# Decay attention and a two-layer product in one kernel: the order of a job's second product, the distance of a unit's second product, and the queues of loads and stores

## The chip, the cores and the metric

The kernel runs on one core of a Trainium2 chip. The core has five engines, each with an instruction stream of its own that it works through strictly in order: TensorE (PE in the profile; its weight loads are listed apart as PEld), VectorE (DVE), ScalarE (ACT), GpSimd (POOL) and SyncE (SP), which here only issues transfers. Engines wait for each other through semaphores. Transfers are issued by an engine's queue and carried out by 16 DMA engines. The metric is the time of one execution in microseconds (us), lower is better.

## What is computed

The first half is attention with a decay, for 8 batches and 8 heads, 576 positions and a head size of 64; the second half is a two-layer product on the attention's output, with a piecewise quadratic between the layers.

```python
# q, k, v: (8, 8, 576, 64)   f: (8, 8, 576)
scores = np.matmul(q, k.transpose(0, 1, 3, 2)) / np.sqrt(D)
cum = np.cumsum(np.log(np.clip(f, 0.0001, 1.0)), axis=-1)
decay = cum[:, :, :, None] - cum[:, :, None, :]
scores = np.where(causal, -1e9, scores + decay)
attn = softmax(scores)                       # over the last axis
x = np.matmul(attn, v)                       # -> (4608, 512), heads side by side
h = x @ w_in                                 # (4608, 2048)
g = np.where(h >= 1, h, np.where(h <= -1, 0.0, (h + 1) ** 2 / 4))
out = g @ w_out                              # (4608, 512)
```

Inputs and outputs are float32. The kernel splits most operands of its matmuls into a high and a low float16 part and sums three products, high by high, low by high and high by low.

## The kernel before, in words

**Jobs.** The attention is cut into 36 jobs. A job is two heads of one batch and a range of query tiles of 128 rows. Batch 0 has eight jobs, four with the tiles 0 and 1 and four with the tiles 2 to 4; each of the other seven batches has four jobs with all five tiles (28 jobs). The first 12 jobs (`NQK`) and the first 5 (`NPE`) take simpler paths for scores and for weights; what follows is the general one.

- `load` (L326) brings the queries and keys of a job's two heads into one of two buffers, `qk32[ji % 2]` (L347, L351). `load_decay` (L355) brings the running sums of the decay, `ck` (L358).
- `measure` (L390) sums the squares of queries and keys on ACT (L397) and turns them into scales by a tiny matmul (L128) and a few VectorE instructions.
- `prepare` (L408) makes the float16 parts `qs` on ACT (L414) and VectorE (L416), which reads the buffer for the last time, and turns them by a DMA transpose (L421) into `qkT`.
- `scores` (L459) multiplies one query tile with all its keys (L482); POOL makes the decay and the causal mask (L488, L492).
- `weights` (L557) adds, takes the exponential and the sum (L571, L575), divides and splits into `pr` (L589, L595), and turns `pr` by DMA transposes into the job's `pT` (L601; L604 for the last tile). `pT` has one buffer.
- `split_values` (L427) brings the job's values into `v32` (L440, L442) and makes their float16 parts `vs` (L447, L448), in two buffers.
- `values` (L608), the job's second product, multiplies `pT` with `vs` (L615) and writes the result into `x` (L624, L625).

**The loop** (from L759) opens job p with the load of pair p+2, prepares pair p+1 and computes the scores of the first tile. Then come the steps. A step (L773) computes the scores of the next tile and the weights of this one; the last but one also brings the next job's values, the last one measures pair p+2. The second product of job p-1 is a step of its own, `finish` (L794), put in by hand: at place 4 where the job has five tiles, which is behind four tiles, otherwise at place 2.

**Units.** The two-layer product runs in units of 256 tokens by 256 hidden columns, 18 chunks of tokens with 8 units each. `moe_front` (L642) makes 24 to 48 matmuls into `ph` (L657), and then `u` and `g`: L666 and L667 on ACT, L668 on VectorE, L670 on ACT, L671 on VectorE. `moe_back` (L678) makes the second product, twelve matmuls into the two halves of `po` (L685); after the last unit of a chunk `po` is copied to `ot` (L702) and stored (L705). `ph` and `g` have two buffers each, the halves of `po` one each. `moe_unit` (L710) emits the front of a unit and the back of the unit before. Units are spread over the steps of a job by a quota.

**The order on each engine.** The program is written down in the order above, but the launch code builds it with `schedule_with_timeline_sim=True`: a scheduler simulates it at build time, and puts on each engine's stream what its own times see ready first, the earlier written one where several are ready. An engine's stream is therefore fixed at build, with later jobs' instructions moved ahead into gaps. On the chip an engine still takes it strictly in order. SP's queue holds all transfers, stores included.

Of the kernel before, what the change touches and what calls it, by code (L numbers as in the profile page):

```python
# [8 lines left out]
F32 = mybir.dt.float32  # L9
F16 = mybir.dt.float16  # L10
I32 = mybir.dt.int32
AF = mybir.ActivationFunctionType
ALU = mybir.AluOpType
AX = mybir.AxisListType

P = 128
# [29 lines left out]
def kernel(  # L46
# [19 lines left out]
    nc = tc.nc  # L66

    B, H, S, D = q.shape
    DM, DF = w_in.shape
    NPAIR = H // 2  # L70
    NT5 = -(-S // P)
# [6 lines left out]
    TC = 256  # L78
    NCH = B * S // TC
    jobs = [(b, hp, r0, r1) for b in range(B) for r0, r1 in CUTS.get(b, ((0, NT5),)) for hp in range(NPAIR)]  # L80
    njobs = len(jobs)
# [65 lines left out]
    def decay_sums():  # L147
        fl = early
        nb = B * H
        nc.sync.dma_start(fl[0:nb, 0:S], f.rearrange("b h s -> (b h) s"))  # L150
        nc.vector.tensor_scalar(
            out=fl[0:nb, 0:S], in0=fl[0:nb, 0:S], scalar1=1e-4, scalar2=1.0, op0=ALU.max, op1=ALU.min
        )
        nc.scalar.activation(fl[0:nb, S:2 * S], fl[0:nb, 0:S], AF.Ln)
        nc.gpsimd.memset(fl[0:nb, 3 * S:4 * S], 0.0)
        cum = fl[0:nb, 2 * S:3 * S]
        nc.vector.tensor_tensor_scan(
            out=cum, data0=fl[0:nb, S:2 * S], data1=fl[0:nb, 3 * S:4 * S], initial=0.0, op0=ALU.add, op1=ALU.add
        )
        nc.sync.dma_start(cum_d, cum)  # L160
        pt = ps.tile([P, 1024], F32, name="s")
        twice = fl[0:nb, 0:P]
        nc.vector.tensor_copy(
            twice.rearrange("p (a b) -> p a b", a=2), cum[:, FULL:S].unsqueeze(1).broadcast_to([nb, 2, 64])
        )
        for t in range(NT5):
            nc.tensor.transpose(
                pt[:, nb * t:nb * t + nb], cum[:, P * t:P * t + P] if t < LAST else twice, ident[0:nb, 0:nb]
            )
        nc.vector.tensor_copy(cq.rearrange("p t n -> p (t n)"), pt[:, 0:NT5 * nb])  # L170

# [193 lines left out]
    early_qk = [two.tile([P, 4, SP], F16, name="qkT") for i in range(2)]  # L367
    early_qk = [t.rearrange("p c s -> p (c s)").bitcast(F32)[:, 0:2 * S].rearrange("p (c s) -> p c s", c=2) for t in early_qk]
    squares = bits.bitcast(F16)[:, 0:2 * NT5 * D]
    cq8 = const.tile([P, NT5, 2 * H], F32, name="cq8")  # L370

    def early_prepare(w):

        if w.p == 0:
            nc.vector.tensor_scalar(out=cq8, in0=cq[:, :, 0:2 * H], scalar1=8.0, scalar2=None, op0=ALU.mult)
        t_ = early_qk[(w.p + NQK) % 2]
        w.nsig, w.nalpha = -8.0, -0.125
        bh = w.b * H + 2 * w.hp
        w.cqs = cq8[:, :, bh:bh + 2]
        w.terms = ((t_[:, 0], t_[:, 1]),)  # L380
        for j in range(2):
            pt = ps.tile([P, 1024], F32, name="s")
            t0 = 0 if j else w.r0
            n = w.s1 - P * t0
            for c0 in range(0, n, P):
                m = min(P, n - c0)
                nc.tensor.transpose(pt[:, c0:c0 + m], w.x32[j][0:m, c0:c0 + P], ident[0:m, 0:m])
            nc.scalar.activation(t_[:, j, 0:n], pt[:, 0:n], AF.Copy)

    def measure(w):  # L390

        if w.p < NQK:
            return
        bh = w.b * H + 2 * w.hp
        m2 = tiny.tile([P, 2], F32, name="m2q")
        for j in range(2):
            nc.scalar.activation(squares, w.x32[j], AF.Square, accum_out=m2[:, j:j + 1])  # L397
        w.sc = sc = tiny.tile([P, 2], F32, name="sc")
        pw = tiny.tile([P, 2], F32, name="pw")
        from_norms(sc, pw, m2)  # L400
        w.nsig = tiny.tile([P, 1], F32, name="nsig")
        nc.vector.tensor_scalar(out=w.nsig, in0=sc[:, 0:1], scalar1=sc[:, 1:2], scalar2=-8.0, op0=ALU.mult, op1=ALU.mult)
        w.nalpha = tiny.tile([P, 1], F32, name="nalpha")
        nc.vector.tensor_scalar(out=w.nalpha, in0=pw[:, 0:1], scalar1=pw[:, 1:2], scalar2=-0.125, op0=ALU.mult, op1=ALU.mult)
        w.cqs = tiny.tile([P, NT5, 2], F32, name="cqs")
        nc.vector.tensor_scalar(out=w.cqs, in0=cq[:, :, bh:bh + 2], scalar1=w.nsig, scalar2=-1.0, op0=ALU.mult, op1=ALU.mult)

    def prepare(w):  # L408
        if w.p < NQK:
# [232 lines left out]
    def moe_front(ch, fb):  # L642
        g0 = ch * TC
        b0 = g0 // S
        n0 = min(TC, (b0 + 1) * S - g0)
        segs = [(0, n0, b0, g0 - b0 * S)] + ([(n0, TC, b0 + 1, 0)] if n0 < TC else [])
        last = segs[-1][2]
        if (ch, fb) not in bsc and last not in bsc:
            bsc[last] = moe_scales(last)
        z = bsc.get((ch, fb)) or bsc[last]  # L650
        i = fb - z.first
        ph = ps.tile([P, 2, TC], F32, name="ph")
        for fi in range(2):
            for t in range(NKT):
                for wl, xl in ((0, 0), (0, 1), (1, 0)):
                    for a0, a1, b, s0 in segs:
                        nc.tensor.matmul(  # L657
                            ph[:, fi, a0:a1],
                            lhsT=wi[fb][:, wl, t, fi * P:(fi + 1) * P],
                            rhs=xs[b][:, t, xl, s0:s0 + a1 - a0],  # L660
                            start=(fi == 0 and t == 0 and wl == 0 and xl == 0 and a0 == 0),
                            stop=(fi == 1 and t == NKT - 1 and wl == 1 and a1 == TC),
                        )
        h = ph.rearrange("p f t -> p (f t)")
        u = two.tile([P, 2 * TC], F32, name="u")
        nc.scalar.activation(u, h, AF.Relu, scale=z.u[:, i:i + 1], bias=z.h[:, i:i + 1])  # L666
        nc.scalar.activation(u, u, AF.Square)  # L667
        nc.vector.scalar_tensor_tensor(out=u, in0=h, scalar=z.t[:, i:i + 1], in1=u, op0=ALU.max, op1=ALU.min)  # L668
        g = two.tile([P, 2, 2 * TC], F16, name="g")
        nc.scalar.activation(g[:, 0], u, AF.Copy, scale=z.r[:, i:i + 1])  # L670
        nc.vector.scalar_tensor_tensor(  # L671
            out=g[:, 1], in0=u, scalar=z.r[:, i:i + 1], in1=g[:, 0], op0=ALU.mult, op1=ALU.subtract
        )
        return ch, fb, g, z

    ots = {}

    def moe_back(ch, fb, g, z):  # L678
        first, last, part = z.first == fb, z.last == fb, z.first > 0
        if first:  # L680
            po[ch] = [ps1.tile([P, DM], F32, name=f"po{i}") for i in range(2)]
        for fi in range(2):
            for i in range(2):
                for gl, wl in ((0, 0), (0, 1), (1, 0)):
                    nc.tensor.matmul(  # L685
                        po[ch][i],
                        lhsT=g[:, gl, fi * TC + i * P:fi * TC + (i + 1) * P],
                        rhs=wo[fb][:, wl, fi, :],
                        start=(first and fi == 0 and gl == 0 and wl == 0),
                        stop=(last and fi == 1 and gl == 1),  # L690
                    )
        if not last:
            return
        if not part:
            ots[ch] = [two.tile([P, DM], F32, name="ot") for i in range(2)]
        for i in range(2):
            if part:
                nc.vector.scalar_tensor_tensor(
                    out=ots[ch][i], in0=po[ch][i], scalar=z.osc, in1=ots[ch][i], op0=ALU.mult, op1=ALU.add
                )  # L700
            else:
                nc.scalar.activation(ots[ch][i], po[ch][i], AF.Copy, scale=z.osc)  # L702
            if fb == NB - 1:
                tok = ch * TC + i * P
                nc.sync.dma_start(out[tok:tok + P, :], ots[ch][i])  # L705


    pending = []

    def moe_unit(ch, fb):  # L710
        pending.append(moe_front(ch, fb))
        if len(pending) > 1:
            moe_back(*pending.pop(0))

    units = [(ch, fb) for ch, first, end in EARLY for fb in range(first, end)]
# [40 lines left out]
        value_step(0, i)  # L756
    value_scale(0)
    split_values(pairs[0])
    for p in range(njobs + 1):  # L759
        w = pairs[p] if p < njobs else None  # L760
        nxt = pairs[p + 1] if p + 1 < njobs else None
        steps = []
        if w:
            if w.b not in xs:
                xs[w.b] = xpool.tile([P, NPAIR, 2, S], F16, name="x")
            if p + 2 < njobs:
                pairs.append(load(p + 2))
            if nxt:
                load_decay(nxt, 0)
                prepare(nxt)  # L770
# [2 lines left out]
            def step(r):  # L773
                if r + 1 < w.r1:
                    scores(w, r + 1)
                if r == w.r1 - 2 and nxt:
                    load_decay(nxt, 1)
                    split_values(nxt)
                weights(w, r)
                if w.r1 == NT5 and w.b + 1 < B:  # L780
                    n = w.r1 - w.r0
                    i = w.hp * n + r - w.r0 - (NPAIR - 1) * n + -(-(NPAIR + 1) // n) * n
                    if 0 <= i <= NPAIR:
                        value_step(w.b + 1, i)
                    if w.hp == NPAIR - 1 and r == w.r0:
                        value_scale(w.b + 1)
# [4 lines left out]
        if p > 0:  # L791
# [7 lines left out]
                        join_scales(wp.b - 1)  # L799
                    tokens = wp.b * S + wp.s1  # L800

            steps.insert(4 if len(steps) == NT5 else 2, finish)
        load_weights(LOADS.get(p, 0))
        blocks = CONVERT.get(p, 0)
        quota = -(-ready() // (NPAIR - (p + NPAIR - 1) % NPAIR))
# [45 lines left out]
```

## Time and profile before

| | us |
|---|---|
| median of 3 runs | 1209.1 (1208.8 to 1213.09) |
| the profiled execution | 1206.77 |
| its span, first to last instruction | 1205.0 |
| TensorE busy | 1047.8 (87%) |
| ACT busy | 795.6 (66%) |
| VectorE busy | 789.7 (66%) |
| GpSimd busy | 418.1 (35%) |

A row of the waits names the waiting engine, its tile and line, then who released it, the total in us, how often, and the longest. A row of the timeline has start, duration, engine, line, what is written from what, how many instructions were merged, and in brackets how long the engine stood before and who ended it. `SPq` is SP's queue, whose durations are the time that issuing took. Every slice of the page has the clock granted to TensorE in tenths of full speed: nine tenths or more after the first fifth of the span, six to nine tenths in it.

### The profile page before, as it was taken

How to read it: one execution, taken by the hardware profiler on the slowest of the kernel's cores; microseconds unless marked ns; L12 is line 12 of the kernel's file. 1: busy time of each engine (PE TensorE's matmuls, PEld its weight loads, DVE VectorE, ACT ScalarE, POOL GpSimd, SP SyncE). 2: the span in 40 equal slices, each digit the busy share in tenths (PEclk: the TensorE clock that was granted, in tenths of full speed). 3: DMA queues.
4: the chain of work that ended last, by engine and by line, in shares of the span. 5: the costliest groups of instructions: out<-in, count | busy, mean ns of one | idle time of the engine just before them, and what ended most of it. 6: DMA issues, size and time to landing. Idle time of an engine off the chain costs nothing. (4 is left out here: it accounts for less than half of the span.)

```text
span 1205.0 us, 24383 instructions
## 1 busy us (share of the span) xinstructions
PE 1047.8 (87%) x8809; PEld 664.8 (55%) x8809; DVE 789.7 (66%) x2103; ACT 795.6 (66%) x1638; POOL 418.1 (35%) x679
## 2 busy tenths in 40 slices
PE   4666765988978889898898998999898999999998
PEld 2433443554645556555655655555565566667665
DVE  5769989787767667765566666676677686532222
ACT  4566876577867677776566667777677686644443
POOL 4467764234533233333213323342343343100000
PEclk9666888998989999998999999999899999999999
DMA  7868788479857566854633745675668575300000
GB/s 226 271 173 243 166 208 180 111 160 181 170 118 169 113 134 127 155 112 111 126 69 76 144 87 130 117 155 116 129 127 149 106 139 105 73 19 1 18 18 18
DMA packets 408281, 152.18 MB, mean 126 GB/s; under 512 B 383968, under 2 KB 384992, under 8 KB 408160
## 3 DMA queue, kind: packets, MB, share of 16 engines
q1 hardware_dynamic: 408160, 150.63, 57.7%
q8 instruction: 69, 1.13, 0.4%
q14 instruction: 52, 0.43, 0.1%
HBM read 75.64 MB, written 9.58 MB: 71 GB/s over the span
## 5 line engine op out<-in xcount | busy, mean ns | idle before, releaser
L685 PE MATMUL po<-place,g 128*128 128x512 f16 x1728 | 429.5, 393 | 55.0 <-ACT g L670 39.4
L657 PE MATMUL ph<-x,place 128*128 128x256 f16 (+3 forms) x4608 | 420.7, 248 | 24.0 <-DVE u L668 24.0
L657 PEld LDWEIGHTS <-place 128*128 128x128 f16 x4608 | 354.2, 98 | 94.2 <-issue 38.5
L685 PEld LDWEIGHTS <-g 128*128 128x128 f16 x1728 | 165.0, 100 | 245.2 <-ACT g L670 56.3
L488 POOL TENSOR_SCALAR sdr<-ck,nsig,cqs 128x128 f32<-128x128 f32 (+1 forms) x192 | 147.3, 771 | 151.2 <-DVE pr L595 148.7
L575 ACT ACTIVATE sdr<-sdr,nm 128x384 f32<-128x384 f32 (+1 forms) x248 | 137.9, 557 | 75.9 <-DVE nm L571 75.3
L668 DVE SCALAR_TENSOR_TENSOR u<-ph,z,u 128x512 f32<-128x512 f32 x136 | 101.6, 747 | 129.4 <-ACT u L667 129.2
L488 POOL TENSOR_SCALAR sd<-ck,nsig,cqs 64x576 f32<-64x576 f32 x48 | 44.2, 921 | 341.6 <-ACT sdr L575 191.6
L666 ACT ACTIVATE u<-ph,z 128x512 f32<-128x512 f32 x136 | 104.4, 768 | 88.0 <-PE ph L657 88.0
L482 PE MATMUL s<-qkT 64*64 64x512 f16 (+11 forms) x1056 | 129.6, 351 | 35.3 <-DVE nm L571 24.9
L595 DVE SCALAR_TENSOR_TENSOR pr<-sdr,rc,pr 128x384 f16<-128x384 f32 (+2 forms) x232 | 129.9, 596 | 41.1 <-ACT pr L589 40.1
L670 ACT ACTIVATE g<-u,z 128x512 f16<-128x512 f32 x136 | 97.8, 719 | 79.0 <-DVE u L668 76.1
L671 DVE SCALAR_TENSOR_TENSOR g<-u,z,g 128x512 f16<-128x512 f32 x136 | 108.0, 794 | 56.6 <-ACT g L670 56.2
L589 ACT ACTIVATE pr<-sdr,rc 128x384 f16<-128x384 f32 (+1 forms) x236 | 118.5, 554 | 10.9 <-issue 6.5
L571 DVE CUSTOM_DVE_ANT_0 sdr<-s,sdr,nalpha 128x128 f32<-128x128 f32 (+1 forms) x192 | 99.4, 545 | 15.9 <-POOL sdr L492 14.6
L492 POOL TENSOR_SCALAR_AFFINE_SELECT sdr<-sdr 128x128 f32<-128x128 f32 x248 | 91.0, 379 | 9.0
L667 ACT ACTIVATE u<-u 128x512 f32<-128x512 f32 x144 | 89.9, 624 | 2.6
L397 ACT ACTIVATE bits<-qk 128x640 f16<-128x640 f32 x48 | 35.0, 729 | 76.1 <-DMA qk<-in_q_dram 75.5
L615 PE MATMUL s<-pT,vs 128*64 128x320 f16 (+3 forms) x1098 | 76.2, 287 | 4.9 <-DMA pT<-pr 4.3
L583 DVE TENSOR_SCALAR rc<-sm 128x2 f32<-128x2 f32 (+1 forms) x149 | 25.9, 174 | 74.4 <-ACT sdr L575 68.4
L615 PEld LDWEIGHTS <-vs 128*64 128x64 f16 x1098 | 50.1, 113 | 33.2 <-issue 15.9
L488 POOL TENSOR_SCALAR sdr<-ck,cq 128x384 f32<-128x384 f32 (+3 forms) x56 | 45.0, 804 | 61.5 <-DVE pr L595 30.2
(155 smaller groups left out, 989.8 us busy)
## 6 DMA issues: line engine op xcount, KB each, us to landing
ck<-cum_d SPq DMA_DIRECT2D x64, 288.0 KB, 3.9
out_dram<-ot SPq DMA_DIRECT2D x36, 256.0 KB, 2.1
qk<-in_k_dram SPq DMA_DIRECT2D x64, 128.0 KB, 3.2
vst<-in_v_dram SPq DMA_DIRECT2D x28, 288.0 KB, 3.2
v<-in_v_dram SPq DMA_DIRECT2D x62, 128.0 KB, 2.7
qk<-in_q_dram SPq DMA_DIRECT2D x56, 128.0 KB, 2.8
place<-in_moe_w_in_dram SPq DMA_DIRECT2D x6, 1024.0 KB, 7.0
place<-in_moe_w_out_dram SPq DMA_DIRECT2D x5, 1024.0 KB, 8.1
```

The lines of the kernel that those rows point to most:

```text
L482: nc.tensor.matmul(sds[h % len(sds)][1][p0:p1, c0:c1], lhsT=a[rows, q0 - w.s0:q0 - w.s0 + p1 - p0], rhs=b[rows, c0:c1], start=(i == 0), st ...
L488: nc.gpsimd.tensor_scalar(out=sd[p0:p1, 0:wid], in0=w.ck[h][p0:p1, 0:wid], scalar1=w.nsig if w.p < NQK else w.nsig[p0:p1], scalar2=w.cqs[p ...
L571: nc.vector.tensor_tensor_reduce(out=a, in0=sp[:, 0:wid], in1=a, scale=w.nalpha, scalar=BIG, op0=ALU.add, op1=ALU.min, accum_out=nm[:, i:i ...
L575: nc.scalar.activation(a, a, AF.Exp, bias=nm[:, i:i + 1], scale=-1.0, accum_out=sm[:, i:i + 1])
L589: nc.scalar.activation(pr[:, :, 0, i, :], a, AF.Copy, scale=rc[:, i:i + 1])
L595: nc.vector.scalar_tensor_tensor(out=pr[:, :, 1, i, :], in0=a, scalar=rc[:, i:i + 1], in1=pr[:, :, 0, i, :], op0=ALU.mult, op1=ALU.subtract,)
L615: nc.tensor.matmul(av[64 * h:64 * h + 64, at + s0:at + s1], lhsT=w.vs[:, vl, h, t, :], rhs=w.pT[:, t, pl, h, s0:s1], start=(t == 0 and pi ...
L657: nc.tensor.matmul(ph[:, fi, a0:a1], lhsT=wi[fb][:, wl, t, fi * P:(fi + 1) * P], rhs=xs[b][:, t, xl, s0:s0 + a1 - a0], start=(fi == 0 and ...
L666: nc.scalar.activation(u, h, AF.Relu, scale=z.u[:, i:i + 1], bias=z.h[:, i:i + 1])
L668: nc.vector.scalar_tensor_tensor(out=u, in0=h, scalar=z.t[:, i:i + 1], in1=u, op0=ALU.max, op1=ALU.min)
L671: nc.vector.scalar_tensor_tensor(out=g[:, 1], in0=u, scalar=z.r[:, i:i + 1], in1=g[:, 0], op0=ALU.mult, op1=ALU.subtract)
L685: nc.tensor.matmul(po[ch][i], lhsT=g[:, gl, fi * TC + i * P:fi * TC + (i + 1) * P], rhs=wo[fb][:, wl, fi, :], start=(first and fi == 0 and ...
```

## The change

- The running sums `cq` are multiplied by 8 when they are copied out of PSUM; the table `cq8` for the first jobs is gone, and the later jobs' factor is -0.125 instead of -1.
- `load` is called for pair 2 ahead of the loop, and for pair p+3 in job p behind the weights of its first tile, instead of for pair p+2 at the opening of job p.
- `finish` is always put at place 1, behind the first tile's step.
- `g` has three buffers, and the back of a unit is emitted two units behind its front.
- The back's loops are exchanged: all six matmuls of the first half of `po`, then all six of the second.
- The stores of the output are issued by ACT's queue.

```diff
-        nc.vector.tensor_copy(cq.rearrange("p t n -> p (t n)"), pt[:, 0:NT5 * nb])
+        nc.vector.tensor_scalar(
+            out=cq.rearrange("p t n -> p (t n)"), in0=pt[:, 0:NT5 * nb], scalar1=8.0, scalar2=None, op0=ALU.mult
+        )
...
-    cq8 = const.tile([P, NT5, 2 * H], F32, name="cq8")
...
-        if w.p == 0:
-            nc.vector.tensor_scalar(out=cq8, in0=cq[:, :, 0:2 * H], scalar1=8.0, scalar2=None, op0=ALU.mult)
...
-        w.cqs = cq8[:, :, bh:bh + 2]
+        w.cqs = cq[:, :, bh:bh + 2]
...
-        nc.vector.tensor_scalar(out=w.cqs, in0=cq[:, :, bh:bh + 2], scalar1=w.nsig, scalar2=-1.0, op0=ALU.mult, op1=ALU.mult)
+        nc.vector.tensor_scalar(out=w.cqs, in0=cq[:, :, bh:bh + 2], scalar1=w.nsig, scalar2=-0.125, op0=ALU.mult, op1=ALU.mult)
...
-        g = two.tile([P, 2, 2 * TC], F16, name="g")
+        g = two.tile([P, 2, 2 * TC], F16, name="g", bufs=3)
...
-        for fi in range(2):
-            for i in range(2):
+        for i in range(2):
+            for fi in range(2):
...
-                nc.sync.dma_start(out[tok:tok + P, :], ots[ch][i])
+                nc.scalar.dma_start(out[tok:tok + P, :], ots[ch][i])
...
-        if len(pending) > 1:
+        if len(pending) > 2:
             moe_back(*pending.pop(0))
...
     split_values(pairs[0])
+    pairs.append(load(2))
     for p in range(njobs + 1):
...
-            if p + 2 < njobs:
-                pairs.append(load(p + 2))
...
                 weights(w, r)
+                if r == w.r0 and p + 3 < njobs:
+                    pairs.append(load(p + 3))
...
-            steps.insert(4 if len(steps) == NT5 else 2, finish)
+            steps.insert(1, finish)
```

## The prediction, made before the result was known

> **What bounds the kernel now.** I read the windows first, to split the span into stages; their columns are the window, its length, the busy time of PE, PEld, DVE, ACT and POOL, the granted TensorE clock, the DMA share and GB/s.
>
> ```profile
> 0.00:210.00 210.00, 132.48 (x759) 80.16 (x759) 172.53 (x429) 140.72 (x301) 127.20 (x173) 0.80 0.80 210
> 210.00:960.00 750.00, 674.69 (x5912) 423.22 (x5913) 508.77 (x1454) 523.68 (x1109) 263.30 (x458) 0.96 0.63 127
> 960.00:1050.00 90.00, 90.00 (x903) 58.23 (x901) 65.58 (x165) 66.18 (x137) 27.65 (x48) 1.00 0.60 115
> 1050.00:1205.00 155.00, 150.67 (x1238) 103.17 (x1236) 42.80 (x57) 65.05 (x93) 0.00 (x0) 1.00 0.04 15
> ```
>
> Up to 210 us DVE is the fullest engine and TensorE stands half the time. From 960 TensorE is full at clock 1.00: nothing is to be had there except less work, and the change takes no matmul away. Between lie 750 us in which TensorE stands 750 - 674.69 = 75.3 us, and whose clock of 0.96 costs about 674.69 x 0.04 = 27 us more. These 102 us are what this change can win. The waits of that stretch say who holds TensorE (total, times, longest):
>
> ```profile
> PE po L685 <- ACT g L670: 33.2, 15, 6.3
> PE ph L657 <- DVE u L668: 23.7, 15, 4.6
> PE po L685 <- ACT ot L702: 14.7, 4, 4.3
> ...
> ACT bits L397 <- DMA qk<-in_q_dram: 75.5, 21, 5.4
> ```
>
> All three wait for the chain L666, L667, L668, L670 of a unit, or for the output copy L702, on ACT and DVE. ACT itself stands 75.5 us in 21 pieces of 3.6 us for the queries that the measuring of a later pair reads. The timeline joins the two: L397 starts 4.02 us late, the unit's chain is queued behind it, and TensorE waits 2.61 us for g.
>
> ```profile
> 944.15 0.74 ACT L397 ACTIVATE bits<-qk 128x640 f16<-128x640 f32 x1 [4.02 <-DMA qk<-in_q_dram]
> ...
> 947.93 0.75 DVE L668 SCALAR_TENSOR_TENSOR u<-ph,z,u 128x512 f32<-128x512 f32 x1 [1.26 <-ACT u L667]
> 948.72 0.72 ACT L670 ACTIVATE g<-u,z 128x512 f16<-128x512 f32 x1 [0.82 <-DVE u L668]
> ...
> 949.49 4.23 PE L685 MATMUL po<-place,g 128*128 128x512 f16 x12 [2.61 <-ACT g L670]
> ```
>
> That is the last L397 wait of the run. In 960 to 1050 attention and units run beside each other as before, without it, and TensorE is full: the bound of the middle is TensorE plus one ACT stall per job.
>
> **The loads, part one of the change.** The code asks for pair p+3 in job p instead of p+1. I do not believe that they come sooner. By 826 us the trace has these counts:
>
> ```profile
> L397 ACT ACTIVATE bits<-qk x40: 718/735/738, 196.6 to 821.3; 128x640 f16<-128x640 f32 x40
> ...
> L414 ACT ACTIVATE qs<-qk,sc x36: 812/813/827, 245.3 to 806.3; 128x640 f16<-128x640 f32 x36
> ```
>
> Two instructions a pair: 20 pairs measured, 18 prepared. The pair measured at 817 to 821 us is the second after the one being prepared, so it has the same one of the two qk32 buffers; the scheduler had already moved its load up to the point where L416 lets go of that buffer. The new code can't pass that point. I take 0 for the place of the loads itself; if the wait at L397 went entirely, all 102 us would come back (a rival below).
>
> **The product of job p-1, part two.** Here is one job on all queues:
>
> ```profile
> 828.49 2.25 PE L615 MATMUL s<-pT,vs 128*64 128x64 f16 x36
> ...
> 830.77 6.78 SPq L601 DMA_TRANSPOSE pT<-pr  x4
> ...
> 833.41 0.87 DVE L595 SCALAR_TENSOR_TENSOR pr<-sd,rc,pr 128x640 f16<-128x640 f32 x1
> ...
> 836.10 0.67 PE L482 MATMUL s<-qkT 64*128 64x128 f16 x12
> ...
> 836.70 2.79 PE L657 MATMUL ph<-x,place 128*128 128x256 f16 x24
> ...
> 837.97 2.69 SPq L604 DMA_TRANSPOSE pT<-pr  x2
> ...
> 840.24 1.68 DVE L416 SCALAR_TENSOR_TENSOR qs<-qk,sc,qs 128x640 f16<-128x640 f32 x2 [0.35 <-ACT qs L414]
> 840.72 1.17 SPq L440 DMA_DIRECT2D v<-in_v_dram  x2
> ...
> 842.68 1.08 SPq L347 DMA_DIRECT2D qk<-in_q_dram  x2
> ...
> 843.86 4.51 SPq L421 DMA_TRANSPOSE qkT<-qs  x1
> ...
> 849.04 0.63 SPq L351 DMA_DIRECT2D qk<-in_q_dram  x1
> ```
>
> The single pT buffer is free only after L615, so four row transposes stand on SP until 830.77 and then go in a burst with the two of the last row, the value loads, the query loads and the 4.51 us transpose L421; the last query part, L351, on which L397 waits, is issued at 849.04. With L615 behind the next job's first query tile, the row transposes leave one by one. The first half of L416 ended at 840.24 + 0.84 = 841.1; an SP without the burst issues the queries then, and L421 after 1.08 us at 842.2 instead of 843.86: 1.7 us sooner, and so does the wait at L397. TensorE's waits at ph and ot get shorter by up to that much: four of 1.7 for ot, 7; for ph, whose 15 waits average 1.6, I take 10. Together -17. The ends: 0, if SP stays as late, and -38 (23.7 + 14.7), if they go. The nearest row is the 1.7.
>
> What it adds: L615 must now have the last row's transposes (L604), and TensorE takes its instructions in order; scores, units and all else stand behind it.
>
> ```profile
> L604 SPq DMA_TRANSPOSE pT<-pr x62: 1207/1282/2904, 109.6 to 1046.2; - x62
> ...
>   PE s L615: 4.3, 3
> ...
> DMA to landing us min/median/max: 3.0/3.3/8.1
> ```
>
> In the job shown the row is ready at 834.28; free of the burst, L604's second issue is at 835.6 and lands at 838.9. The scores of the next two tiles end at 836.77: going straight to L615 would cost 2.1 us. With one front (836.70, 2.79 us) between, TensorE comes at 839.5 and waits nothing. The ends are 0 and 28 x 2.1 = 59 us over the 28 five-row jobs; I take +10, nearer to none, because a unit belongs to almost every step.
>
> **The second product two units behind, and g with three buffers, part three.** Today TensorE runs front n+1, then needs g of n. Now it runs back n-1 in between, and the next thing of unit n that it needs is its ph buffer, for front n+2. One back is 2.59 us, and ph is free (L668 ends at 948.68) 0.8 us before the matmul of g starts at 949.49. So a g wait of W becomes W - 3.4.
>
> ```profile
> 965.82 2.59 PE po L685 x12
> ...
> 340.16 1.89 PE L685 MATMUL po<-place,g 128*128 128x512 f16 x4 [6.25 <-ACT g L670]
> ...
> 405.31 1.03 PE L685 MATMUL po<-place,g 128*128 128x512 f16 x2 [3.48 <-ACT g L670]
> ...
> 693.98 0.82 PE L685 MATMUL po<-place,g 128*128 128x512 f16 x3 [4.12 <-ACT g L670]
> ```
>
> Only these three are longer than 3.4; they leave 2.9 + 0.1 + 0.7 = 3.7, and 33.2 - 3.7 = 29.5 us go. The ends: 0, if fronts and not backs are what TensorE asks for first, and -33.2. What is late next is ph, whose two buffers are unchanged. At the end of the run the last g wait (0.5) goes as well. The loop order of the back (i outside) completes the first half of po six matmuls sooner and asks for the second half six later; L702 stands behind L397 all the same when ot is late, so 0 beyond the above.
>
> **Stores on ACT, cq, and the start.**
>
> ```profile
> SPq L601 <- PE s L615: 174.7, 16, 20.4
> SPq L705 <- ACT ot L702: 56.7, 14, 13.6
> ...
> L705 SPq DMA_DIRECT2D out_dram<-ot x36: 332/338/917, 228.6 to 1201.9; - x36
> ...
> L375 DVE TENSOR_SCALAR cq<-cq x1: 236/236/236, 10.0 to 10.0; 128x80 f32<-128x80 f32 x1
> ```
>
> The 36 stores take 36 x 0.34 = 12 us of ACT's time, behind copies that ACT has just made; ACT is busy 523.68 of 750 us, so I take 0, at worst +12. SP no longer stands 4 us a time for ot. The Trainium skill, "DMA: Bandwidth & Descriptors", section "Issuing engines are not separate DMA queues", says that issuing from several engines only saves the issuing sequencer's time, which is usually small. By that the store edit is worth nothing; by the wait row it frees SP 56.7 us, which is a stand in the queue and not issue time. The sum holds 0 for it either way. The removed scaling L375 is 0.24 us of DVE, once. In the first 210 us weights and early jobs are spread over DVE, SP and ACT; the order moves, no large operation goes: 0, between -8 and +8.
>
> **The clock.** After the stall above the granted clock fell:
>
> ```profile
> 948.00:952.00 4.00, 2.51 (x9) 0.96 (x10) 2.77 (x6) 1.80 (x4) 0.16 (x1) 0.86 0.01 4
> 952.00:956.00 4.00, 4.00 (x35) 1.62 (x34) 2.58 (x6) 2.99 (x7) 1.32 (x3) 0.71 0.00 0
> ```
>
> Twelve matmuls took 4.23 us that take 2.59 at full clock. I let the 27 us shrink with the idle time: 75.3 - 29.5 - 17 + 10 = 38.8 stay, so 36.5/75.3 x 27 = 13 us come back (0 to 27). The Trainium skill, "TensorE: Matmul & The Clock Gate", section "What's actually happening", lets the clock halve after an idle window of about 3.4 us. By that only the few longest waits cost clock and some 6 us, as an estimate, would come back instead of 13; the trace disagrees, since 2.61 us sufficed here.
>
> **Sum.** -29.5 - 17 + 10 - 13 - 0.5 = -50 us. The profiled execution took 1206.8 us (span 1205.0), so 1157; the median of the runs, 1209.1, lies 2.3 higher: **1159 us**. Its own range, with the ends of the added wait and of the ph and ot terms, is 1130 to 1185.
>
> **Rivals.**
> *The L397 wait vanishes* (the earlier place does help): idle and clock loss of the middle go, -75.3 - 27 - 0.5, 1106 us. For it stands the full stretch after 960; against it the shared buffer.
> *The lag gives nothing:* TensorE asks for ph first, and the g waits return there at full length; the 15 ph waits show that this order occurs. Left are 17 us and 17/75.3 x 27 = 6 of clock: 1186 us.
> *The change does not do what it says:* loads at the buffer's limit, SP as late as now, waits only renamed: 1209 us.
> *The product in front of its transposes (slower):* the mechanism is L615 after the scores with no front between, 2.1 us in each of 28 jobs. Every us of it costs 28 x (1 + 27/75.3) = 38 us with its clock. Without it the change wins 29.5 + 17 + 0.5 + 46.5/75.3 x 27 = 63.7 us, so it decides from 1.7 us a job; at 2.1 it is 80 - 63.7 = 16 us slower: 1225 us. For it: the scheduler puts instructions where its own times see data ready, and L397 shows those early by 3.6 us. Against it: so far L615 waited for these transposes three times, 4.3 us in all.
>
> **Chances.** Forecast 0.50, wait vanishes 0.10, lag gives nothing 0.14, nothing done 0.11, product too early 0.15. A measurement of this kernel can tell some 0.5% (6 us) from no change: faster 0.74 (the first three), same 0.11, slower 0.15. The range reaches from part of the best case to just short of the slow one: 1118 to 1214.
>
> **What would show it.** Right: the PE wait for g near zero in the middle, ph waits no larger than now; row transposes spread over a job on SP; L421 right behind L416; L397 waits still there, once a job, some 2 us; clock 0.98. Wrong: waits of L615 for pT of 2 us a job (the slow rival); ph waits of 40 us and more (the lag gives nothing); no L397 waits (loads did come sooner); ACT waits or stalls behind its own stores.

## The result, and the profile after

The changed kernel takes **1137.9 us** (median of 4 runs, 1134.75 to 1142.58) against 1208.95 us (4 runs of the kernel before, 1205.07 to 1213.09): 0.9415 of it, interval 0.9368 to 0.9463, 71 us less. Forecast were 50 us less, with a range that holds the time. The profiled execution took 1136.2 us with a span of 1134.4.

The windows again (columns as in the prediction). The middle ends 70 us sooner, so the cuts lie at 890 and 980. Lines from L375 on have one number less than before: L397 is now L396, L615 L614, L657 L656, L685 L684.

```profile
0.00:210.00 210.00, 134.72 (x751) 82.04 (x752) 161.96 (x408) 135.42 (x287) 124.47 (x163) 0.77 0.77 203
210.00:890.00 680.00, 658.40 (x5928) 424.68 (x5926) 514.90 (x1473) 525.26 (x1121) 268.93 (x464) 0.99 0.66 144
890.00:980.00 90.00, 88.89 (x923) 59.37 (x922) 65.13 (x165) 66.99 (x139) 32.00 (x52) 1.00 0.47 105
980.00:1135.00 155.00, 150.32 (x1219) 102.28 (x1214) 42.83 (x57) 65.10 (x93) 0.00 (x0) 1.00 0.04 15
```

The cuts leave the first and last stages as long as before (210 and 155 us). In the middle TensorE stands 680 - 658.40 = 21.6 us instead of 75.3, and its clock of 0.99 costs some 7 us instead of 27. That is 54 + 20 = 74 us; 1.1 us more idle between 890 and 980, and a first stage that does less work at a lower clock (134.72 x 0.77 = 103.7 against 132.48 x 0.80 = 106.0), take some 3 back.

The waits of 210 to 960 us (total, times, longest), where g stood at 33.2, ph at 23.7 and ot at 14.7:

```profile
PE s L614 <- DMA pT<-pr: 11.6, 13, 2.7
PE s L481 <- DVE nm L570: 3.9, 4, 2.0
PE s L614 <- DVE nm L570: 3.4, 6, 1.2
PE ph L656 <- DVE u L667: 2.5, 1, 2.5
...
ACT bits L396 <- DMA qk<-in_k_dram: 18.2, 14, 2.4
ACT bits L396 <- DMA qk<-in_q_dram: 16.7, 14, 2.6
```

g and ot are gone from the list, ph is a tenth. (4.3 of the 23.7 us at ph lay ahead of the window: the first of these waits ran from 205.7 to 210.3 us.) What is new is the product L614 waiting for its row transposes. ACT's wait at the measuring has halved, 76 to 34.9 us, and none of its pieces is longer than 2.6. One job on SP, by the timeline (start, length, what is issued):

```profile
626.57 2.54 SPq L603 DMA_TRANSPOSE pT<-pr  x2
630.60 0.94 SPq L349 DMA_DIRECT2D qk<-in_q_dram  x2
631.64 3.65 SPq L420 DMA_TRANSPOSE qkT<-qs  x1
635.34 0.63 SPq L353 DMA_DIRECT2D qk<-in_q_dram  x1
...
641.67 2.94 SPq L600 DMA_TRANSPOSE pT<-pr  x2
```

The burst is gone: the row transposes (L600, L603) are spread, and L420 leaves as soon as the queries before it have left: over the middle it starts 0.3 us behind the last L415 ahead of it, in the median, where L421 started 2.3 us behind L416 in the kernel before. The query loads still stand beside L420 of the pair being prepared, as forecast; they did not move a job ahead.

### The profile page after: what moved, and what is told of

Read it like the earlier page. It is cut to its first block, busy times and chain, and to the rows that moved or that the text cites. A ratio compares the mean times of both kernels' runs of the same rounds, so it can differ in the third digit from the quotient of the medians.

```text
span 1134.4 us, 24411 instructions
## 1 busy us (share of the span) xinstructions
PE 1032.3 (91%) x8809; PEld 668.4 (59%) x8809; DVE 784.8 (69%) x2102; ACT 792.8 (70%) x1638; POOL 425.4 (38%) x679
## 5 line engine op out<-in xcount | busy, mean ns | idle before, releaser
L656 PE MATMUL ph<-x,place 128*128 128x256 f16 (+3 forms) x4608 | 415.8, 248 | 6.0 <-DVE u L667 6.0
L684 PE MATMUL po<-place,g 128*128 128x512 f16 x1728 | 403.1, 382 | 2.2 <-DVE g L670 1.7
L656 PEld LDWEIGHTS <-place 128*128 128x128 f16 x4608 | 352.0, 99 | 66.1 <-issue 25.6
L684 PEld LDWEIGHTS <-g 128*128 128x128 f16 x1728 | 166.4, 99 | 180.0 <-issue 5.5
L594 DVE SCALAR_TENSOR_TENSOR pr<-sdr,rc,pr 128x384 f16<-128x384 f32 (+2 forms) x232 | 124.8, 571 | 37.4 <-ACT pr L588 34.4
L481 PE MATMUL s<-qkT 64*64 64x512 f16 (+11 forms) x1056 | 122.8, 346 | 17.8 <-ACT qkT L387 10.5
L670 DVE SCALAR_TENSOR_TENSOR g<-u,z,g 128x512 f16<-128x512 f32 x136 | 102.6, 756 | 46.5 <-ACT g L669 44.1
L487 POOL TENSOR_SCALAR sd<-ck,nsig,cqs 64x576 f32<-64x576 f32 x48 | 58.0, 1208 | 157.1 <-DMA ck<-cum_d 106.2
L614 PE MATMUL s<-pT,vs 128*64 128x64 f16 (+3 forms) x1098 | 83.5, 290 | 30.3 <-DMA pT<-pr 22.2
L614 PEld LDWEIGHTS <-vs 128*64 128x64 f16 x1098 | 58.9, 114 | 57.5 <-issue 36.4
L491 POOL TENSOR_SCALAR_AFFINE_SELECT sdr<-sdr 128x128 f32<-128x128 f32 x248 | 79.5, 332 | 10.2
L481 PEld LDWEIGHTS <-qkT 64*128 64x128 f16 (+1 forms) x864 | 31.7, 98 | 56.3 <-issue 42.1
L396 ACT ACTIVATE bits<-qk 128x640 f16<-128x640 f32 x48 | 35.2, 733 | 35.2 <-DMA qk<-in_k_dram 18.2
```

The lines of the kernel that those rows point to most:

```text
L481: nc.tensor.matmul(sds[h % len(sds)][1][p0:p1, c0:c1], lhsT=a[rows, q0 - w.s0:q0 - w.s0 + p1 - p0], rhs=b[rows, c0:c1], start=(i == 0), st ...
L487: nc.gpsimd.tensor_scalar(out=sd[p0:p1, 0:wid], in0=w.ck[h][p0:p1, 0:wid], scalar1=w.nsig if w.p < NQK else w.nsig[p0:p1], scalar2=w.cqs[p ...
L594: nc.vector.scalar_tensor_tensor(out=pr[:, :, 1, i, :], in0=a, scalar=rc[:, i:i + 1], in1=pr[:, :, 0, i, :], op0=ALU.mult, op1=ALU.subtract,)
L614: nc.tensor.matmul(av[64 * h:64 * h + 64, at + s0:at + s1], lhsT=w.vs[:, vl, h, t, :], rhs=w.pT[:, t, pl, h, s0:s1], start=(t == 0 and pi ...
L656: nc.tensor.matmul(ph[:, fi, a0:a1], lhsT=wi[fb][:, wl, t, fi * P:(fi + 1) * P], rhs=xs[b][:, t, xl, s0:s0 + a1 - a0], start=(fi == 0 and ...
L670: nc.vector.scalar_tensor_tensor(out=g[:, 1], in0=u, scalar=z.r[:, i:i + 1], in1=g[:, 0], op0=ALU.mult, op1=ALU.subtract)
```

## The experiments

The theory was the prediction's: one ACT stall a job, at the measuring, is the source of the g, ph and ot waits; the lag covers g, the early product frees SP. The rivals: SP's queue is the source, or each part hides what another already hides. Ratios are against runs of the kernel before on the same chip (medians 1211.3, 1211.6 and 1210.4 in the three groups e1 to e4, e5 to e8, e9 to e12). Waits are those of 210 to 960 us.

### The parts alone

**e1: the lag alone**, with g's third buffer and the edit of cq, which makes room for it.

```diff
+        g = two.tile([P, 2, 2 * TC], F16, name="g", bufs=3)
-        if len(pending) > 1:
+        if len(pending) > 2:
```

> The kernel before with the lag alone: back two units behind its front, g in three buffers, and cq scaled once so that the buffer fits. My theory (one back of 2.6 us more between a front and the need of its g): the g waits of TensorE fall from 33 to under 5 us between 210 us and the end of the attention, the ACT waits at L397 stay at some 75 us, the ph waits stay at some 24 and the ot waits at some 15; 1209 - 29.5 - 29.5/75.3 x 27 = about 1169 us. Rival (SP's burst does it, through the wait at L397): 1195 to 1209. Rival (the g waits return at ph): ph waits above 45 us, 1200 to 1209.

1144.6 us, 0.9448 (0.9394 to 0.9502): 67 us from this part alone, where 40 were expected. TensorE's waits:

```profile
PE ph L656 <- DVE u L667: 21.2, 15, 4.6
...
PE po L684 <- ACT ot L701: 3.0, 2, 2.1
PE po L684 <- ACT g L669: 2.2, 7, 0.4
```

The timeline of one long ACT wait (in brackets at the end of its row), and of TensorE under it:

```profile
885.85 0.74 ACT L396 ACTIVATE bits<-qk 128x640 f16<-128x640 f32 x1 [2.92 <-DMA qk<-in_q_dram]
...
885.45 2.75 PE L684 MATMUL po<-place,g 128*128 128x512 f16 x12
888.14 0.93 PE L481 MATMUL s<-qkT 64*64 64x512 f16 x12
889.37 2.32 PE L614 MATMUL s<-pT,vs 128*64 128x64 f16 x36 [0.30 <-DMA ck<-cum_d]
891.62 2.79 PE L656 MATMUL ph<-x,place 128*128 128x256 f16 x24
894.25 2.75 PE L684 MATMUL po<-place,g 128*128 128x512 f16 x12
```

ACT stands 2.92 us and TensorE 0.30: the back that it takes at 885.45 has had its g since 882.3. g fell by 31.0 (29.5 forecast) and ph stayed (23.7 to 21.2), both as predicted. Not predicted: ot fell from 14.7 to 3.0, ACT's wait at L396 from 76.1 to 54.7, and the clock rose to 0.99 with half of the idle time still there. SP still stands 188 us for the product and ot, 231 before:

```profile
SPq L600 <- PE s L614: 98.7, 13, 19.4
SPq L704 <- ACT ot L701: 89.2, 21, 17.1
```

Why ot fell shows in ACT's order. In the kernel before, all four copies for which TensorE waited came behind an L397 that had stood 3.2 to 3.9 us since the chunk's last back; one of them:

```profile
727.57 0.74 ACT L397 ACTIVATE bits<-qk 128x640 f16<-128x640 f32 x1 [3.92 <-DMA qk<-in_q_dram]
...
732.05 0.67 ACT L702 ACTIVATE ot<-po,z 128x512 f32<-128x512 f32 x1
...
732.77 2.72 PE L685 MATMUL po<-place,g 128*128 128x512 f16 x6 [4.34 <-ACT ot L702]
```

In e1 no copy in the middle has a waiting L396 between the last back and itself. The scheduler has placed them otherwise; why isn't shown.

**e2: the early product alone.**

```diff
-            steps.insert(4 if len(steps) == NT5 else 2, finish)
+            steps.insert(1, finish)
```

> The kernel before with the second product of job p-1 put behind the first query tile of job p, alone. My theory (row transposes no longer wait on SP for it): the ACT wait at L397 falls from 3.6 us a job to under 2, all three kinds of TensorE waits shrink by up to 1.7 us each, some 10 us of new waits of the product for its transposes; about 1209 - 37 + 11 - 9 = 1174 us. Rival (the lag does it all): 1200 to 1212. Rival (product too early): product waits of 50 us or more, 1215 to 1230.

1180.1 us, 0.9738 (0.9686 to 0.9791): 31 us. The waits of TensorE, and ACT's at L397:

```profile
PE po L685 <- ACT g L670: 14.8, 12, 2.8
PE ph L657 <- DVE pw L129: 9.8, 5, 3.3
PE s L615 <- DMA pT<-pr: 9.4, 9, 1.9
PE ph L657 <- DVE u L668: 8.6, 9, 3.5
...
ACT bits L397 <- DMA qk<-in_q_dram: 52.3, 20, 4.3
ACT bits L397 <- DMA qk<-in_k_dram: 24.5, 15, 4.6
```

The step that I gave for it falls: ACT waits as long at L397 as before (76.8 us against 76.1). But it waits in 35 pieces of 2.2 us instead of 21 of 3.6, and TensorE's waits for g, u and ot, 71.6 us before, are 23.4, with 19.2 of new ones for pw and pT. A stall cut in two would cost less than one if each piece meets the same slack of the unit's chain. That this is what happened isn't tested, nor why the stall is cut (the key loads now wait in their turn, by their row). The price of the early product is the row with pT: 9.4 us.

**e3: lag and early product together**, without the new place of the loads, the loop order and the stores on ACT.

> Both together, without the loads, the loop order and the ACT stores. My theory: these two are nearly all of the change, 1138 to 1150 us. Rival (ACT stores or the loop order clear the ot waits, which are then still 10 to 15 us here): 1152 to 1165.

1137.4 us, 0.9389 (0.9333 to 0.9445): the whole change, within the error. TensorE's waits:

```profile
PE s L614 <- DMA pT<-pr: 10.3, 12, 2.4
PE s L614 <- DVE nm L570: 4.2, 4, 1.1
```

g and ot don't appear; these are nearly the rows of the changed kernel, with 52.8 us of waits at L396 instead of its 34.9. Loads, loop order and store queue add nothing that can be measured beside the other two.

**e4: the loads alone.**

```diff
+    pairs.append(load(2))
-            if p + 2 < njobs:
-                pairs.append(load(p + 2))
                 weights(w, r)
+                if r == w.r0 and p + 3 < njobs:
+                    pairs.append(load(p + 3))
```

> The kernel before with the loads alone: pair 2 ahead of the loop, pair p+3 in job p. My theory (they already stood at the point where the buffer comes free): 1209 within 6 us, L397 waits of 70 to 80 us, the same order on SP in the middle. Rival (they come sooner): L397 waits under 20 us, 1130 to 1185 us.

1195.4 us, 0.986 (0.9805 to 0.9915): 16 us, a small gain whose interval stops short of 1, where the prediction had 0. SP's timeline behind L421 in the kernel before, then that of e4:

```profile
719.73 3.38 SPq L421 DMA_TRANSPOSE qkT<-qs  x1
723.21 0.53 SPq L358 DMA_DIRECT2D ck<-cum_d  x1
723.79 0.63 SPq L351 DMA_DIRECT2D qk<-in_q_dram  x1
```

```profile
715.89 3.32 SPq L421 DMA_TRANSPOSE qkT<-qs  x1
719.26 0.63 SPq L351 DMA_DIRECT2D qk<-in_q_dram  x1
...
721.82 1.01 SPq L358 DMA_DIRECT2D ck<-cum_d  x2
```

The loads are still behind L421, as forecast, but they have passed the load of ck. ACT's wait at L397 fell from 76.1 to 62.5 us. That this half microsecond of queue is all of the 16 us isn't shown; that the gain is covered by the lag and the early product is (e3).

### The source of the waits

**e5: the kernel before, with the measuring held back.** A write of m2 that needs the job's last row sum keeps the scheduler from placing L397 ahead of it; m2 is overwritten by what follows.

```diff
-    def measure(w):
+    def measure(w, rc):
...
         m2 = tiny.tile([P, 2], F32, name="m2q")
+        nc.vector.tensor_scalar(out=m2, in0=rc[:, 0:1].broadcast_to([P, 2]), scalar1=0.0, scalar2=None, op0=ALU.mult)
...
+        w.rc = rc
...
-                    measure(pairs[p + 2])
+                    measure(pairs[p + 2], w.rc)
```

> The kernel before, with the measuring of a pair tied to the last tile's sum of the job in which it is written: one tiny VectorE instruction writes m2 from that sum first, so the scheduler can't move L397 ahead to where the queries have just been asked for. Lag, product, loads and stores are those of before. My theory (the ACT wait at L397 is what all three TensorE waits come from): L397 waits under 5 us in all, g, ph and ot waits under 20 us together between 210 us and the end of the attention instead of 72; about 1209 - 60 - 20 = 1130 us, at most 1150. Rival (the chains are late by themselves, and the lag is needed): L397 waits gone, g and ph waits still 40 us or more, 1175 to 1205.

1145.3 us, 0.9456 (0.9422 to 0.9489): as much as the lag, with nothing of the change in it. TensorE's waits, and SP's for the product and ot (the new lines shift the numbers: L482 is L483 here, L657 L659, L670 L672, L685 L687):

```profile
PE s L483 <- DVE nm L572: 13.3, 5, 5.6
PE po L687 <- ACT g L672: 7.1, 7, 3.3
PE ph L659 <- DVE u L670: 6.1, 7, 1.4
...
SPq L603 <- PE s L617: 158.2, 21, 17.9
SPq L707 <- ACT ot L704: 26.1, 13, 7.0
```

ACT's wait for the queries is gone, and the g, ph and ot waits fall from 71.6 to 13.2 us, while SP still stands 158.2 us for the product and 26.1 for ot (174.7 and 56.7 before). So the stall at L397 is the source of most of them, and the product's stand on SP is not; the stand for ot halved here, but in e1 it grew to 89.2 us and the g and ot waits went all the same. The timeline of the kernel before agrees: 61.3 of the 71.6 us come within 9 us behind an L397 wait, all of g and ot, and 13.4 of ph; the other ten ph waits, 10.3 us, have none within 18 us. The edit also lets the scheduler order the rest anew, so a share of the 66 us can be due to that. This is the rival "the L397 wait vanishes", brought about by another edit.

**e6: the same in the changed kernel.**

> The changed kernel with the same late measuring. My theory (its cushion already swallows the 35 us of L397 waits that are left): 1138 within 8 us. Rival (they still cost): 1115 to 1128.

1134.8 us, 0.9369 (0.9336 to 0.9401), no difference from the changed kernel that can be told. Its 34.9 us of ACT waits cost next to nothing: the lag swallows them.

**e8: the changed kernel with a lag of one.**

```diff
-        if len(pending) > 2:
+        if len(pending) > 1:
```

> The changed kernel with the back one unit behind its front again (g keeps three buffers). Lag alone gave 0.945 and the product's place alone 0.974 of the time before. My theory (both take the same waits away, so what the lag adds to the rest is less than what it gives alone): g waits of some 10 to 20 us, 1155 to 1180 us. Rival (the parts add up): 1195 to 1205, the lag worth its 65 us here too.

1148.5 us, 0.9479 (0.9444 to 0.9514), g waits of 3.7 us. Inside the change the lag is worth 11 us by the medians and 8 by the ratios, whose intervals overlap; alone it is worth 67. I had expected more of it here. The parts do not add: 67 + 31 + 16 = 114 us alone, 71 together, because each takes away the same waits.

### The place of the product, and the stores

**e7 and e9: the changed kernel with the product at place 2 and at place 3** of the five-row jobs.

```diff
-            steps.insert(1, finish)
+            steps.insert(min(2, len(steps)), finish)
```

> The changed kernel with the second product of job p-1 behind two query tiles instead of one. My theory: its waits for its transposes, 11 us in the middle, go to under 3, the row transposes wait a little more on SP: 1125 to 1136. Rival (transposes held back cost as much): 1138 within 5.

> The changed kernel with the product behind three query tiles in jobs of five, behind two otherwise. Place 1 gave 1138, place 2 1120 us. My theory (place 2 already leaves the transposes time; each later place holds the row transposes on SP longer): 1118 to 1130. Rival (later is better still, toward place 4): under 1114.

Place 2: 1120.1 us, 0.9254 (0.9213 to 0.9296), with 3.4 us of pT waits, faster than expected. Place 3: 1141.4 us, 0.9424 (0.9397 to 0.9452), slower than expected, without pT waits, but with these instead:

```profile
PE s L481 <- DVE nm L570: 15.1, 22, 2.4
PE ph L656 <- DVE u L667: 15.0, 12, 4.1
```

The price of place 1 is real: TensorE's wait for the transposes falls from 11.6 to 3.4 us with one step more between. It explains 8 of the 18 us that place 2 wins. Place 3 should then have been as good and is 21 us worse. The two rows shown are 1.4 and 5.4 us at place 2, so these waits, 23 us more, make up the difference; that they come from the new order that the scheduler makes of everything after each edit is likely and not shown.

**e10: place 2 with the measuring held back.**

> The changed kernel with the product at place 2 and the late measuring. My theory (13 us of L397 waits are left there and the two units of cushion cover them): 1120 within 6. Rival (they still cost): 1105 to 1113.

1130.4 us, 0.9339 (0.9309 to 0.9369): 10 us slower than e7 where no difference was expected. Its longest row of TensorE's waits is one that e7 doesn't have (L397 here is the changed kernel's L396):

```profile
PE ph L128 <- ACT bits L397: 7.7, 5, 4.0
```

TensorE now waits for the measuring itself: held back, it comes late for its pair.

**e11: place 2, stores back on SP and the old loop order.**

```diff
-        for i in range(2):
-            for fi in range(2):
+        for fi in range(2):
+            for i in range(2):
-                nc.scalar.dma_start(out[tok:tok + P, :], ots[ch][i])
+                nc.sync.dma_start(out[tok:tok + P, :], ots[ch][i])
```

> The changed kernel with the product at place 2, stores issued by SP again and the loop over the halves of po inside again. My theory (neither is on the path): 1120 within 6. Rival (stores held SP and ot held TensorE): 1128 to 1145, with ot waits of 5 us and more or SP waits for ot ahead of the transposes.

1122.8 us, 0.9283 (0.9241 to 0.9326), against e7's 0.9254: nothing that can be told. The Trainium skill, "DMA: Bandwidth & Descriptors", section "Issuing engines are not separate DMA queues", expects little of such an edit; this pair of runs agrees, at 3 us.

**e12: the kernel before with e1's and e5's edits only**: the lag, and the measuring held back. Product, loads, stores and loop order are the old ones.

> The kernel before with the lag and the late measuring, product at place 4, loads and stores as before. The lag alone gave 0.945, the late measuring alone 0.946 of the time before. My theory (both remove the same waits, one by cushion, one at the source; what is left of ph waits, 21 us under the lag, goes): 1118 to 1132. Rival (they add up): under 1100.

**1113.2 us**, 0.9188 (0.9164 to 0.9212): faster than both kernels, 25 us under the changed one, and 5 under the range expected. The window of its middle, and the waits in 210 to 960 us:

```profile
210.00:870.00 660.00, 648.14 (x5936) 420.94 (x5935) 524.21 (x1480) 521.79 (x1110) 269.03 (x458) 1.00 0.66 146
```

```profile
PE s L482 <- DVE nm L571: 3.9, 2, 3.4
PE po L686 <- ACT g L671: 3.2, 3, 1.9
```

TensorE stands 11.9 us in the middle, at clock 1.00. The source is away, what is left meets the cushion, and the product keeps the place that costs no wait for transposes. SP still stands 88.0 us for the product and 62.0 for ot there, at no price.

## Why the prediction was right, and where it was wrong

**The bound: right in the main.** TensorE waited for an ACT stall at L397 once a job; e5 removes the stall and 58 of the 72 us of waits go. "All three wait" was too wide for ph: only 13.4 of its 23.7 us come behind an L397 wait.

**The g waits, -29.5: right.** They went (33.2 to nothing; 31.0 less in e1), and the fronts did not take the waits over: ph stayed at 21.2 in e1. The rival "the lag gives nothing" is out.

**The new wait of L615, +10: right.** 11.6 us. The front between the scores and the product was mostly there. That the size came so near is luck: +10 was a choice between 0 and 59. The slow rival needed 1.7 us in each of 28 jobs; the row shows 13 waits of 0.9.

**ph and ot, -17: the mis-sized term.** They fell by 23.7 + 14.7 - 2.5 = 35.9 us, the far end that I had named. Two steps failed. "So does the wait at L397", shorter by 1.7 us a job because SP is free of its burst: the burst went, L421 left 2 us earlier, and the wait at L397 was as long as before in e2; what changed was the length of its pieces. And "L702 stands behind L397 all the same when ot is late, so 0": in e1 the copies no longer stood behind a waiting L396, and the lag alone took ot from 14.7 to 3.0. I gave the lag nothing of ot.

**The clock, -13: the second mis-sized term**, 20 measured. I let the loss shrink in proportion to the idle time. The traces' records of the granted clock show why that fails. They come in steps of 3.41 us, at 1.00 or 0.50. Before, the falls that begin in 210 to 960 us hold 54.6 us of half clock, 27 us of loss; e1, with half of the idle, holds 10.2; the changed kernel holds 13.7. (The page of the kernel before shows them: four of its slices after the first fifth of the span are at eight tenths, not at nine or more.) Two such steps of the kernel before in which TensorE stood long, each with the step behind it (windows cut to the steps; the granted clock is the third number from the end):

```profile
759.75:763.17 3.42, 0.75 (x11) 0.41 (x8) 0.43 (x3) 3.42 (x10) 0.65 (x2) 1.00 0.32 98
763.17:766.58 3.41, 3.41 (x12) 1.09 (x13) 3.41 (x6) 3.38 (x6) 1.97 (x2) 0.50 0.00 0
916.77:920.18 3.41, 1.48 (x26) 1.17 (x23) 1.48 (x4) 3.41 (x10) 0.49 (x1) 1.00 0.09 33
920.18:923.59 3.41, 2.15 (x20) 1.85 (x19) 2.67 (x5) 3.41 (x7) 1.54 (x5) 1.00 0.44 158
```

The step with 3.42 - 0.75 = 2.67 us idle is followed by half clock, the one with 1.93 is not. In this middle all 12 steps with 2.0 us or more of idle were followed by half clock, and of the full-clock steps with less only one, with 1.87. Over the middles of all 14 traces, every full-clock step with 2.0 us or more was followed by half clock; between 1.7 and 2.0 both occur. What counts, by these, is the idle time inside one step. In the kernel before it was mostly one long wait, and a cushion that shortens such waits brings the clock back at once. But 6 of its 17 waits of 2 us and more, up to 3.2 us long, cost no clock, since they lay across two steps, as one of 3.2 us that begins at 918.25 us does, in the third and fourth of the rows shown; and two of the changed kernel's four falls follow steps in which shorter waits added up to 2 us. The Trainium skill, "TensorE: Matmul & The Clock Gate", section "What's actually happening", puts the fall after an idle window of about 3.4 us in a grid that runs by itself. I set it aside because a stall of 2.61 us sufficed. The steps agree with its window; that a window with some 2 us of idle counts as idle is what the runs add. My estimate by that section, 6 us, was further off than the 13.

**The loads, 0: the order was right, the price not.** They came no job sooner, but e4 won 16 us alone. In the sum the 0 did no harm, as e3 shows.

**Stores, loop order, cq, start: 0 each, right** to within what can be measured (e3, e11).

The sum thus reads -33 - 36 + 12 - 20 = -77 for the middle; against it stand the 4 us of ph that lay ahead of it, and 3 of the other stages. The range held the time, but not by the parts as I had sized them: ph and ot gave 19 us more than I had put and the clock 7, and the lag alone gave nearly the whole of it. The signs that were named came true, but for the L396 waits: 28 of 1.2 us instead of one a job of 2.

**Where the gain stands in the middle.** Idle time of TensorE and half of its time at half clock (falls that begin in the window), 210 to 960 us of one profiled execution, in us, beside what the median gained on the kernel before:

| | idle | clock loss | less than before by | gain |
|---|---|---|---|---|
| before | 75.3 | 27.3 | | |
| e4 | 63.3 | 27.3 | 12 | 16 |
| e2 | 48.4 | 10.2 | 44 | 31 |
| e1 | 38.1 | 5.1 | 59 | 67 |
| e9 | 35.2 | 5.1 | 62 | 69 |
| e5 | 28.6 | 8.5 | 65 | 66 |
| e3 | 25.4 | 8.5 | 69 | 74 |
| e10 | 21.0 | 10.2 | 71 | 80 |
| e6 | 18.6 | 11.9 | 72 | 77 |
| changed | 22.7 | 6.8 | 73 | 71 |
| e8 | 22.5 | 3.4 | 77 | 63 |
| e11 | 14.1 | 5.1 | 83 | 88 |
| e7 | 12.8 | 3.4 | 86 | 91 |
| e12 | 12.1 | 1.7 | 89 | 97 |

The two last columns agree within 9 us but for e2 and e8, which gained 13 and 14 less than the middle says; TensorE is busy 1045.6 and 1044.3 us in their whole runs, against 1032.3 in the changed kernel, and why is open. **What stays open** besides: why the waits of the three places differ as they do (by the table 13 of the 18 us between places 1 and 2, and all between 2 and 3, are idle and clock), and why held-back measuring helps at place 4 (e12) and hurts at place 2 (e10). Edits that move one instruction changed the time by 10 to 20 us, so one such comparison isn't evidence for a mechanism without its row of waits.

## What to carry to other kernels

Find the in-order engine whose wait starts the others, and try both remedies: take the wait away at its source (a dependency that keeps a scheduler from hoisting an instruction whose data comes late) and run the consumer further behind; here each was worth 66 us alone and both 97. Run each part of a change by itself before pricing the whole, since parts that cure the same wait don't add. And price a stall by its length: one of over 2 us can cost its clock too. Here 11 of the 17 in the kernel before did, while short ones far apart did not.

## What the runs showed of the hardware

- The clock is granted for steps of 3.41 us, and in the middles of these traces a step in which TensorE stands 2 us or more is followed by one or two at half clock: 2.33 us idle at 268 to 272 us in the kernel before were paid with 6.8 us at half clock.
- A transpose of qs (L421) holds SP's queue 3.3 to 4.5 us for one instruction in the rows shown, against 0.6 us for a query load; this is what a load that follows it waits for.
- The output stores landed 3.1 us after their issue from ACT in the changed kernel and 2.1 us from SP in the one before (medians of 36); in e7 and e11, which differ in the stores and the loop order alone, it is 3.0 and 2.6 us, without a difference in the time.
